# One written order for the first two batches of a fused attention, gated convolution and spatial-gating kernel

## The chip, the cores and the metric

The kernel runs on one core of a Trainium2 chip. The metric is the device time of one launch in microseconds (us). The core has a matrix engine (TensorE, "PE" in the profile; its weight loads are "PEld"), a vector engine (VectorE, "DVE"), an activation engine (ScalarE, "ACT"), a general engine (GpSimd, "POOL") and a queue that only issues DMA transfers here (SyncE, "SP"). Each engine works through its own list of instructions in the order of the list and waits on semaphores for the others.

## The reference

Three layers follow each other. Everything is float32, with 8 batches of 576 tokens.

```python
# 1: linear attention, 8 heads of 64
kv  = einsum('bhsd,bhse->bhde', k, v)
out = einsum('bhsd,bhde->bhse', q, kv)
rms = sqrt(mean(out * out, axis=-1, keepdims=True) + 1e-06)
x   = (out / rms * g_norm)            # -> (batch, 576, 512)
# 2: gated projection; the gate is a causal convolution with 5 taps
gate = 1 / (1 + exp(-sum_k conv_w[k] * shifted(x, k)))
y    = (gate * (x @ w_val)) @ w_out
# 3: spatial gating
h = gelu_tanh(y @ w_in);  u, v = split(h)
v_n = (v - mean(v)) / sqrt(var(v) + 1e-06) * g_ln
v_s = einsum('ts,bsd->btd', w_sg, v_n) + b_sg
return y + (u * v_s) @ w_out2
```

## The kernel before

Tokens of a batch are worked in five tiles of 128 (`TOK`; the fifth overlaps the fourth, its last 64 tokens, the "rest", are new). Layers 1 and 2 go batch by batch; layer 3 follows for all batches and is not touched. All matrix products keep float32 accuracy by splitting an operand into a high part (rounded to fp32r) and a low part (what is left): `gemm3` (line 222) makes 12 products of 128x512 for one output block of 128 columns.

One batch of layers 1 and 2 is this chain. `kv` makes the 8 head products k'v, 40 small matmuls; `kv_out` copies them on ACT into the block diagonal tile `kvbd`. For each token tile, `o` (line 291) multiplies q by `kvbd` into a PSUM bank `o`; ACT squares it (line 302); DVE sums over a head (305); GpSimd forms mean plus epsilon (306) and its power -0.5 (307), the "root" of 8 heads per token; DVE multiplies the bank by the root, broadcast over 64 columns (310, the "scale"). `transpose` turns the tile on PE into a bank `xT` (325), ACT writes the high part `X0h` or `X1h` (329) and the full float32 copy `X` (330), DVE the low part (334). `taps` and `conv` build the gate: ACT makes the first tap (353), DVE the other four (359), for each of four blocks of 128 channels; ACT takes the sigmoid (362). `Moe.val` (line 378) makes the product with w_val, DVE multiplies it by the gate (387), ACT writes the high part of `Z` (388), and the low part of `Z` (391) comes from GpSimd for blocks 0 and 2 and from DVE for blocks 1 and 3, save in batch 0, where DVE makes all four. `Moe.out` makes the product with w_out into a bank `y`, ACT copies it (405) and a DMA stores it.

The weights w_val, w_out and conv_w come in as float64 and are unpacked by DVE and ACT (lines 131 to 143); w_val and w_out need three steps more for their low parts, on PE and ACT for five of the eight column pieces (`summed`, tile `l`), on DVE for the other three (lines 186 and 188).

The order of the work is set in two ways. Up to the low parts of batch 0's `Z` it is written out by hand: the block under `tc.manual_schedule()` (line 705), where `busy(n)` puts n dummy matmuls of 128x128 (tile `warm`) on PE. After that, `later` and `tick` say in which slot a piece is due, and a scheduler orders each engine's list. SP's list starts with the four pieces of w_val, one of w_out, k and v of batch 0 in halves, conv_w and q. Batch 1's projections start while batch 0's `y` is under way.

Of the kernel before, what the change touches and what calls it, by code (L numbers as in the profile page):

```python
# [19 lines left out]
P = 128  # L20
# [8 lines left out]
KC = 5  # L29
# [6 lines left out]
ROOM = {"st": 128, "bst": 32, "bmv": 32, "gcol": 32, "gln": 32, "mhalf": 96, "cw": 64, "T": S, "X32": 19 * 128}  # L36
APART = 8

# [27 lines left out]
def body(ctx, tc, qT, k, v, gcol, w_val, conv_w, w_out, w_in, g_ln, w_sgT, b_sg, w_out2, out, out_r):  # L66
# [45 lines left out]
    nc.gpsimd.memset(mhalf, -0.5)  # L112
    kvbd = [sb(f"kvbd{i}", [NK, P]) for i in range(2)]
# [31 lines left out]
    def split(src, h, l, raw=None, tmp=None, k=None, last=nc.gpsimd.tensor_tensor):  # L145
# [20 lines left out]
        def first():  # L166
            if wide:
                st["steps"] = wide_parts(st["raw"].rearrange("p (n t) -> p n t", t=2),
                                         sb("cv", [3, n]) if tmp is None else tmp)
                st["steps"][0]()  # L170

        def steps():

            ops = st["steps"][1]
            yield ops[0]()
            yield ops[1]()
            a = ops[2]()
            act(h, flat(a), AF.Copy)
            yield
            yield ops[3]()  # L180
            c = ops[4]() if last else ops[4](l, flat)
            yield
            if last is None:
                st["parts"] = a, c
                return
            last(flat(a), flat(a), f32(h), op=ALU.subtract)  # L186
            yield
            tt(l, flat(a), flat(c), op=ALU.add)  # L188
            yield

        def summed():

            a, c = st["parts"]
            ps = bank("l", n)
            for i, (w, x) in enumerate(((ident, flat(a)), (signed[:, 1], h), (signed[:, 0], c))):
                nc.tensor.matmul(flat(ps), lhsT=w, rhs=x, start=(i == 0), stop=(i == 2))
            return lambda: act(l, flat(ps), AF.Copy)

        def rest():
            r = st["raw"]  # L200
            if wide:
                for _ in steps():
                    pass
            else:
                act(h, flat(r), AF.Copy)
                tt(l, flat(r), f32(h), op=ALU.subtract)
# [5 lines left out]
        return load, work, first, steps if wide else lambda: iter([rest()]), summed if wide and last is None else lambda: lambda: None  # L212
# [32 lines left out]

    class Attention:
        def __init__(self, b):
            self.b = b
            self.xh, self.xl = (sb(f"X{b % 2}{i}", [NK, MAIN], F32R) for i in "hl")

        def load_kv(self):
            b = self.b
            self.k, self.v = sb("K", [5, D]), sb("V", [5, D])
            for c in (((0, 2), (2, 4)) if b == 0 else ((0, 4),)):
                for t_, src in ((self.k, k), (self.v, v)):
                    dma(t_[:, c[0]:c[1], :], src[b, P * c[0]:P * c[1], :].rearrange("(c p) d -> p c d", p=P))
            dma(self.k[:, 4, :], k[b, TOK[4]:, :])
            dma(self.v[REST:, 4, :], v[b, MAIN:, :])
            nc.gpsimd.memset(self.v[:REST, 4, :], 0.0)

        def load_q(self):
            self.q = sb("Q", [NK, S])
            dma(self.q, qT[self.b].rearrange("m p s -> p m s"))

        def kv(self, half):
            if half == 0:
                if self.b:
                    pk = bank("kv")
# [13 lines left out]
            if half:  # L282
                later(0, self.kv_out, 0)

        def kv_out(self):
            bd = kvbd[self.b % 2]
            for pk, j in self.pk3:
                act(bd[:DH, j, :DH], pk[:DH, :, :DH], AF.Copy)
                act(bd[DH:, j, DH:], pk[DH:, :, DH:], AF.Copy)

        def o(self, t, wait=3):
            bd = kvbd[self.b % 2]
            o = TOK[t]
            po = bank("o")
            for j in range(NK):
                nc.tensor.matmul(po[:, j * P:(j + 1) * P], lhsT=self.q[:, j, o:o + P], rhs=bd[:, j, :], start=True, stop=True)  # L296
            st = sb("st", [3, 8], bufs=5)
            xo = tmp(D)
            x3 = xo.rearrange("p (h d) -> p h d", d=DH)

            def square():
                act(xo, po, AF.Square)

            def norm(small=nc.gpsimd.tensor_scalar):
                nc.vector.tensor_reduce(st[:, 0], x3, axis=AX.X, op=ALU.add)
                small(st[:, 1], st[:, 0], 1.0 / DH, 1e-6, op0=ALU.mult, op1=ALU.add)  # L306
                nc.gpsimd.tensor_tensor(st[:, 2], st[:, 1], mhalf, op=ALU.pow)  # L307

            def scale():
                tt(x3, po.rearrange("p (h d) -> p h d", d=DH),  # L310
                   st[:, 2].unsqueeze(2).to_broadcast([P, 8, DH]), op=ALU.mult)

            if wait is None:
                square()
                return norm, scale, lambda: self.transpose(t, xo, True)
            later(0, square, 0)
            later(0, norm, 0)
            later(wait - 1, scale, 0)
            later(wait, lambda: self.transpose(t, xo), 0)

        def transpose(self, t, xo, apart=False):
            o, n = (TOK[t], P) if t < 4 else (MAIN, REST)
            pt = bank("xT")
            for j in range(NK):
                nc.tensor.transpose(pt[:, j * P:(j + 1) * P], xo[:, j * P:(j + 1) * P], ident)
            pt = pt.rearrange("p (j e) -> p j e", j=NK)[:, :, P - n:]
            if t < 4:
                xh, xl = self.xh[:, :, o:o + n], self.xl[:, :, o:o + n]
                act(xh, pt, AF.Identity, scale=gcol_s)
            act(x32[:, :, HALO + o:HALO + o + n], pt, AF.Identity, scale=gcol_s)  # L330

            def low():
                if t < 4:
                    stt(xl, pt, gcol_s, f32(xh), op0=ALU.mult, op1=ALU.subtract)

            if apart:
                return low
            low()

        def rest_parts(self):  # L340

            if self.b % RG == 0:
                rest["x"] = sb("XR", [2, NK, RW], F32R, o=APART)
                rest["g"] = sb("GR", [NK, RW])
            c = self.b % RG * REST
            xs = x32[:, :, HALO + MAIN:]
            xh, xl = (rest["x"][:, i, :, c:c + REST] for i in range(2))
            act(xh, xs, AF.Copy)
            tt(xl, xs, f32(xh), op=ALU.subtract)
            act(rest["g"][:, :, c:c + REST], gate[:, :, MAIN:], AF.Sigmoid)  # L350

        def taps(self, m):
            act(gate[:, m], x32[:, m, 0:S], AF.Copy, scale=cw3[:, m, 0:1])  # L353

        def conv(self, ms):

            for j in range(1, KC):
                for m in ms:
                    stt(gate[:, m], x32[:, m, j:j + S], cw3[:, m, j:j + 1], gate[:, m], op0=ALU.mult, op1=ALU.add)  # L359
# [11 lines left out]
    class Moe:  # L371


        def __init__(self, xh, xl, g, dst):
            self.xh, self.xl, self.g, self.dst, self.n = xh, xl, g, dst, xh.shape[2]

        def val(self, m, apart=False):
            n = self.n
            if m == 0:
                self.z = sb("Z", [2, NK, n], F32R, o=APART if n == RW else 0)  # L380
            zh, zl = self.z[:, 0, m], self.z[:, 1, m]
            ps = bank("val", n)
            gemm3(ps, (wv[:, 0], wv[:, 1]), m, self.xh, self.xl)
            z = tmp(n)

            def gated():
                tt(z, ps, self.g[:, m, :n], op=ALU.mult)  # L387
                act(zh, z, AF.Copy)

            def low(on_pool=m in (0, 2)):  # L390
                (nc.gpsimd.tensor_tensor if on_pool else tt)(zl, z, f32(zh), op=ALU.subtract)  # L391

            if apart:
                return gated, low
            later(0, gated, 0)
            later(0, low, 0)

        def out(self, m):
            if m == 0:
                self.y = sb("Y", [NK, self.n])  # L400
            ps = bank("y", self.n)
            gemm3(ps, wo, m, self.z[:, 0], self.z[:, 1])

            def done():
                act(self.y[:, m], ps, AF.Copy)
                if m == NK - 1:
                    dma(self.dst, self.y)

            later(0, done, 1)
# [219 lines left out]
    def product():  # L629

        return next(i for i in reversed(nc.cur_bb.bb.instructions) if i.engine == mybir.EngineType.PE)
# [45 lines left out]
    wv_pieces = first_weight((wv[:, 0], wv[:, 1]), w_val, [first[0][:, i] for i in range(4)], tmps, [None] * 4)  # L677
    wo_pieces = first_weight(wo, w_out, [spare[:, 0], spare[:, 1], first[0][:, 0], first[0][:, 1]],
                             tmps[:2] * 2, [None, tt, tt, tt])
    att = Attention(0)  # L680
    atts = [att, Attention(1)]

    def taps():
        if conv_w.dtype == F32:
            dma(cw, conv_w)
            return lambda: None
        raw = sb("raw", [WC * 2], I32, bufs=2)[:, :2 * NK * KC]
        dma(raw, conv_w.bitcast(I32))

        def work():  # L690
            one, ops = wide_parts(raw.rearrange("p (n t) -> p n t", t=2), sb("cv", [3, NK * KC]))
            one()
# [292 lines left out]
```

## Time and profile before

| quantity | value |
|---|---|
| device time, median of 3 runs | 729.43 us (729.15 to 729.48) |
| time of the profiled execution | 727.04 us |
| its span, first to last instruction | 725.2 us |
| PE busy | 709.9 us, 98% |
| DVE busy | 583.6 us, 80% |
| ACT busy | 350.3 us, 48% |
| POOL busy | 152.5 us, 21% |
| granted TensorE clock | 1.000 (2.4 GHz) |

The span lies 1.8 us inside the profiled execution's time, and that execution 2.4 us under the median. Busy time is a sum over stages with different limits; the stretch that the change touches is the first 107 us or so, up to the first projection of batch 2 at 106.81 us. A record "x60" of 128x128 matmuls stands for 30 of them: each float32 product leaves two.

### The profile page before, as it was taken

Reading aid. Unit: us, or ns where it says so; the run is one execution under the profiler, and the core shown is the slowest. Engines: PE = TensorE matmul, PEld = TensorE weight load, DVE = VectorE, ACT = ScalarE, POOL = GpSimd, SP = SyncE. Lnnn points to the kernel's source line nnn. Section 1 sums busy time; section 2 is a strip of 40 time slices with the busy share of each in tenths; the row PEclk is TensorE's granted clock in tenths of the full one; section 3 lists DMA queues with packets and bytes.
Section 4 is the critical chain, followed back from the end, with each engine's and each line's share of the span. In section 5 each row is a group of like instructions: output and inputs, shape, how many; then the busy total and the mean of one; then the engine's idle time right before and its main releaser. Section 6 shows DMA issues by size and latency. Waiting matters only on the chain.

```text
span 725.2 us, 11759 instructions
## 1 busy us (share of the span) xinstructions
PE 709.9 (98%) x4490; PEld 620.7 (86%) x4490; DVE 583.6 (80%) x1127; ACT 350.3 (48%) x667; POOL 152.5 (21%) x173
## 2 busy tenths in 40 slices
PE   8997999999999999999999999999999999999998
PEld 7785888879888888899889889898899898898897
DVE  6699979999989999699976866867856857867662
ACT  4667465676566674475433433424333424334230
POOL 1414437262727361112000000000100000100000
PEclk9999999999999999999999999999999999999999
DMA  9945253525462213433220321122241122111202
GB/s 338 331 141 201 96 195 119 217 80 207 130 251 84 88 30 125 158 120 103 73 81 36 103 89 30 58 88 74 78 156 30 58 88 74 58 59 45 102 1 87
DMA packets 56712, 81.19 MB, mean 112 GB/s; under 512 B 3665, under 2 KB 29265, under 8 KB 55633
## 3 DMA queue, kind: packets, MB, share of 16 engines
q1 hardware_dynamic: 56656, 80.45, 32.2%
q8 instruction: 35, 0.57, 0.3%
q14 instruction: 21, 0.16, 0.1%
HBM read 61.56 MB, written 18.87 MB: 111 GB/s over the span
## 4 chain that ended last, share of the span: by engine, by line
PE 58%; DVE 1%; DMA 0%; ACT 0%; POOL 0%; issue 0%; POOLq 0%; SPq 0%; DVEq 0%
PE sg L587 16%; PE hv L478 14%; PE out L228 14%; PE hu L228 12%; PE hur L228 2%; PE y L228 1%; PE val L228 1%; DMA raw<-y_main 0%; DVE Z L391 0%; DVE T L387 0%; POOL cv L186 0%; DVE cv L134 0%; DVE V L188 0%; DVE cv L141 0%; ACT X1h L455 0%
## 5 line engine op out<-in xcount | busy, mean ns | idle before, releaser
L359 DVE SCALAR_TENSOR_TENSOR G<-X,cw,G 128x576 f32<-128x576 f32 x128 | 98.3, 819 | 5.2 <-ACT G L353 5.1
L228 PE MATMUL y<-Z,WOh 128*128 128x512 f32 (+1 forms) x320 | 96.8, 376 | 0.0
L490 POOL TENSOR_TENSOR bmv<-bmv,mhalf 128x1 f32<-128x1 f32 x36 | 21.4, 596 | 342.6 <-DVE bmv L489 342.6
L478 PE MATMUL hv<-wiv,X1h 128*128 128x512 f32 x256 | 83.1, 390 | 0.1
L228 PE MATMUL out<-Z,K 128*128 128x512 f32 x256 | 83.0, 389 | 0.0
L228 PE MATMUL hu<-X1h,wiu 128*128 128x512 f32 x256 | 79.2, 391 | 0.0
L307 POOL TENSOR_TENSOR st<-st,mhalf 128x8 f32<-128x8 f32 x40 | 70.2, 1762 | 7.0 <-DVE st L306 4.7
L228 PEld LDWEIGHTS y<-Z,WOh 128*128 128x128 f32 x320 | 57.9, 188 | 9.6
L467 ACT ACTIVATE T<-T 128x512 f32<-128x512 f32 x68 | 42.9, 631 | 44.7 <-DVE T L464 44.7
L228 PE MATMUL y<-Z,WOl 128*128 128x512 f32 (+1 forms) x160 | 57.9, 369 | 0.0
L228 PEld LDWEIGHTS out<-Z,K 128*128 128x128 f32 x256 | 48.1, 188 | 10.0
L478 PEld LDWEIGHTS hv<-wiv,X1h 128*128 128x128 f32 x256 | 47.8, 188 | 10.0 <-ACT X1h L455 0.5
L588 DVE SCALAR_TENSOR_TENSOR T<-sg,gln,WOl 128x288 f32<-128x288 f32 x64 | 32.7, 515 | 26.3 <-PE sg L587 26.2
L228 PEld LDWEIGHTS hu<-X1h,wiu 128*128 128x128 f32 x256 | 46.6, 188 | 8.3
L228 PE MATMUL hu<-X1l,wiu 128*128 128x512 f32 x128 | 50.0, 390 | 0.0
L478 PE MATMUL hv<-wiv,X1l 128*128 128x512 f32 x128 | 49.9, 390 | 0.0
L228 PE MATMUL out<-Z,V 128*128 128x512 f32 x128 | 49.8, 389 | 0.0
L599 ACT ACTIVATE Z<-T 128x512 fp32r<-128x512 f32 x32 | 20.1, 630 | 57.5 <-DVE T L598 57.5
L296 PEld LDWEIGHTS o<-kvbd,Q 128*128 128x128 f32 x320 | 40.3, 191 | 2.5 <-issue 0.3
L296 PE MATMUL o<-kvbd,Q 128*128 128x128 f32 x320 | 40.7, 275 | 0.1
L228 PE MATMUL val<-X0h,WV 128*128 128x512 f32 x128 | 40.7, 399 | 0.0
L228 PE MATMUL val<-X1h,WV 128*128 128x512 f32 x128 | 40.6, 398 | 0.0
(174 smaller groups left out, 1699.4 us busy)
## 6 DMA issues: line engine op xcount, KB each, us to landing
Q<-in_qT_dram SPq DMA_DIRECT2D x8, 1152.0 KB, 5.4
y_main<-Y SPq DMA_DIRECT2D x8, 1024.0 KB, 3.8
raw<-y_main SPq DMA_DIRECT2D x32, 256.0 KB, 3.1
Y<-y_main SPq DMA_DIRECT2D x32, 256.0 KB, 4.1
out_dram<-Y SPq DMA_DIRECT2D x32, 256.0 KB, 2.3
K<-in_k_dram SPq DMA_DIRECT2D x7, 1024.0 KB, 5.6
V<-in_v_dram SPq DMA_DIRECT2D x7, 1024.0 KB, 8.5
raw<-in_w_in_dram SPq DMA_DIRECT2D x16, 256.0 KB, 4.7
```

What stands on the lines that cost most here:

```text
L228: nc.tensor.matmul(ps, lhsT=a[:, kt, msl], rhs=x[:, kt], start=(i == 0), stop=(i == 3 * NK - 1))
L296: nc.tensor.matmul(po[:, j * P:(j + 1) * P], lhsT=self.q[:, j, o:o + P], rhs=bd[:, j, :], start=True, stop=True)
L307: nc.gpsimd.tensor_tensor(st[:, 2], st[:, 1], mhalf, op=ALU.pow)
L359: stt(gate[:, m], x32[:, m, j:j + S], cw3[:, m, j:j + 1], gate[:, m], op0=ALU.mult, op1=ALU.add)
L467: act(w, w, AF.Tanh, scale=CG * AG)
L478: nc.tensor.matmul(ps, lhsT=a[:, kt], rhs=p2["wiv"][:, w, kt], start=(i == 0), stop=(i == 3 * NK - 1))
L490: nc.gpsimd.tensor_tensor(mv[:, 3:4], mv[:, 2:3], mhalf[:, 0:1], op=ALU.pow)
L587: nc.tensor.matmul(ps, lhsT=a[:, msl], rhs=w, start=(n == 0), stop=(n == len(mm) - 1))
L588: later(0, lambda: stt(vs[:, sl], ps, gln_s[:, m:m + 1], p2["bsg"][:, sl], op0=ALU.mult, op1=ALU.add))
L599: act(g[:, 0], x, AF.Copy)
```

## The change

The block written by hand is replaced by a string `ORDER` of 356 tokens that are played one after the other, each one instruction or a few, on whichever engine it belongs to. The string reaches further than the old block: over both batches 0 and 1, up to the four `y` products of batch 0 and the low parts of batch 1's `Z`; batch 2's k'v, `o`, scales and transposes are in it too. A token names the step, then batch and tile: `o01` product, `q01` square, `r01` sum, `m01` mean, `w01` root, `s01` scale, `t01` transpose, `h01`, `x01`, `l01` high, full and low copy, `p021` tap 1 of block 2 in batch 0, `v01` the product with w_val, `z01`, `Z01`, `u01` its gated product, high part and low part, `y01` and `Y01` the output product and its copy. `a` and `b` tokens are steps of the weights, `L` tokens loads, `~n` puts n dummy matmuls ahead, and a star chooses the other engine: GpSimd for `m` and `u`, ACT for `s`.

Four things differ in what is done. Ten of the 15 scales in the string run on ACT as 8 activations of 128x64 each, one per head, with the root as the per-partition scale. Seven of the 8 low parts of `Z` of batches 0 and 1 run on GpSimd. Four of the means run on ACT. Four of batch 0's eight copies into `kvbd` run on DVE. There are 37 dummy matmuls in place of 51. Loads move: k and v of batch 0 come behind two pieces of w_val, q of batch 0 in two parts right behind them, the other weight pieces after q; the loads of batches 2 and 3 are issued inside or right at the end of the string, batch 3's q with its k and v.

```diff
+ORDER = """
+W30 La0 La1 LK0a LV0a LK0b LV0b LK0c LV0c Lq0a Lq0b Lg La2 La3 Lb0 Lcw a1a a0a a01 a00 a10 kv0a a02 a11 a12 kv0b a13
...
+p132 w24 t23 b3h b3s s24* w22 t21 p113 p133 s22* b3+ p102 p134 y03 p114 Y02 s20* g1L S11 h23 p103 v10 h21 z11 p104
+z12 l21 Z11 t22 S13 Z12 z13 S10 l23 Z13 h22 t24 z10 u11* t20 Z10 l22 u12* u10 h20 u13* x21 Y03 x23 x24 l20 x22 x20
+g1r
+"""
...
+    def own(ps):
+        for i in range(idle[0]):
+            nc.tensor.matmul(ps[:, :P], lhsT=ident, rhs=ident, start=True, stop=True)
+        idle[0] = 0
+        return ps
...
+        def mean(self, t, by=None):
+            st = self.tile[t]["st"]
+            if by is act:
+                act(st[:, 1], st[:, 0], AF.Identity, scale=1.0 / DH, bias=eps)
+            else:
+                nc.gpsimd.tensor_scalar(st[:, 1], st[:, 0], 1.0 / DH, 1e-6, op0=ALU.mult, op1=ALU.add)
...
+        def scale(self, t, by=None):
+            i = self.tile[t]
+            if by is act:
+                for h in range(8):
+                    act(i["x3"][:, h], i["po"][:, h * DH:(h + 1) * DH], AF.Copy, scale=i["st"][:, 2, h:h + 1])
+                return
+            tt(i["x3"], i["po"].rearrange("p (h d) -> p h d", d=DH),
+               i["st"][:, 2].unsqueeze(2).to_broadcast([P, 8, DH]), op=ALU.mult)
...
+        def low(self, m, on_pool):
             zh, zl = self.z[:, 0, m], self.z[:, 1, m]
...
+            (nc.gpsimd.tensor_tensor if on_pool else tt)(zl, self.t[m], f32(zh), op=ALU.subtract)
...
+        for op in ORDER.split():
+            op, n = (op + "~0").split("~")[:2]
+            idle[0] = int(n)
+            if op[0] == "L":
+                load(op[1:])
+            elif op[0] == "W":
+                busy(int(op[1:]))
+            elif op in ("kv0a", "kv0b"):
+                atts[0].kv("ab".index(op[3]), False)
+            else:
+                act_part(op.rstrip("*"), op[-1] == "*")
+    marks = [latest()] * 4
+    atts.append(Attention(3))
+    atts[3].load_kv()
+    atts[3].load_q()
```

SP's list at the start of the program, before: `wiu` receives w_val, `Y` w_out, `K`, `V` and `Q` are k, v and q of a batch.

```order
L164 DMA wiu_91<-in_w_val_dram 128x4x256 x4
L164 DMA Y_93<-in_w_out_dram 128x4x256
L256 DMA K_106<-in_k_dram 128x2x512
L256 DMA V_107<-in_v_dram 128x2x512
L256 DMA K_106<-in_k_dram 128x2x512
L256 DMA V_107<-in_v_dram 128x2x512
L257 DMA K_106<-in_k_dram 128x512
L258 DMA V_107<-in_v_dram 64x512
L688 DMA raw_115<-in_conv_w_dram 128x40
L263 DMA Q_117<-in_qT_dram 128x4x576
```

SP's list at the start, after:

```order
L183 DMA wiu_93<-in_w_val_dram 128x4x256 x2
L308 DMA K_137<-in_k_dram 128x2x512
L308 DMA V_138<-in_v_dram 128x2x512
L308 DMA K_137<-in_k_dram 128x2x512
L308 DMA V_138<-in_v_dram 128x2x512
L311 DMA K_137<-in_k_dram 128x512
L313 DMA V_138<-in_v_dram 64x512
L320 DMA Q_146<-in_qT_dram 128x4x256
L320 DMA Q_146<-in_qT_dram 128x4x320
```

Two pieces of w_val and the piece of w_out have gone behind q, and the first `o` product needs only q's first part.

ACT's list where batch 1's `Z` is made, before. `G` is the gate, `X0h` and `X` the copies of batch 2's transposed tiles, `T` a temporary, `GR` the rest's gate; line 302 is the square, 362 the sigmoid, 388 the high part of `Z`.

```order
L362 ACTIVATE G_86<-G_86 128x512
L329 ACTIVATE X0h_548<-xT_924,gcol_79 128x4x128
L388 ACTIVATE Z_834<-T_848 128x512
L302 ACTIVATE T_923<-o_917 128x512
L362 ACTIVATE G_86<-G_86 128x512
L330 ACTIVATE X_12_85<-xT_887,gcol_79 128x4x128
L330 ACTIVATE X_12_85<-xT_924,gcol_79 128x4x128
L350 ACTIVATE GR_615<-G_86 128x4x64
L388 ACTIVATE Z_834<-T_879 128x512
L388 ACTIVATE Z_834<-T_916 128x512
L388 ACTIVATE Z_834<-T_956 128x512
```

ACT's list ahead of the same `Z` after; line 385 is the scale, 511 the copy of `y`, 466 the sigmoid, 402 the high copy, 493 the high part of `Z`.

```order
L385 ACTIVATE T_751<-o_732,st_750 128x64 x8
L385 ACTIVATE T_761<-o_701,st_760 128x64 x8
L511 ACTIVATE Y_870<-y_891 128x512
L385 ACTIVATE T_766<-o_745,st_765 128x64 x8
L466 ACTIVATE G_88<-G_88 128x512
L402 ACTIVATE X0h_966<-xT_907,gcol_81 128x4x128
L402 ACTIVATE X0h_966<-xT_923,gcol_81 128x4x128
L493 ACTIVATE Z_990<-T_984 128x512
L466 ACTIVATE G_88<-G_88 128x512
L493 ACTIVATE Z_990<-T_987 128x512
```

All five scales of batch 2's tiles now stand on ACT ahead of batch 1's `Z`; the full copies `X` of batch 2, which stood between, have moved behind it.

## Rows read from the trace of the kernel before

**Rows 1.** Busy time by stretch: start:end, length, us busy (x instructions), clock, DMA.

```profile
0.00:21.86 21.86, 19.46 (x188) 17.24 (x189) 12.53 (x31) 10.70 (x23) 3.22 (x14) 1.00 0.94 333
0.00:93.15 93.15, 84.33 (x759) 72.13 (x759) 79.60 (x142) 56.50 (x106) 32.79 (x41) 1.00 0.62 221
30.00:92.00 62.00, 56.09 (x499) 47.89 (x499) 59.08 (x95) 40.34 (x74) 21.89 (x23) 1.00 0.47 166
106.00:320.00 214.00, 211.05 (x1434) 181.81 (x1433) 199.55 (x362) 131.83 (x255) 94.17 (x91) 1.00 0.38 135
320.00:725.00 405.00, 401.62 (x2237) 356.03 (x2235) 295.87 (x612) 153.01 (x291) 21.86 (x38) 1.00 0.22 72
```

**Rows 2.** PE's waits over the whole span: total us, times, longest.

```profile
PE xT L325 <- DVE T L310: 5.9, 7, 2.9
PE warm L244 <- POOL X L234: 2.3, 1, 2.3
PE xT L325 <- ACT WOh L178: 1.9, 1, 1.9
```

**Rows 3.** Timeline of PE: start, us, instruction, [idle before <- releaser].

```profile
15.02 1.60 PE L244 MATMUL warm<-ident 128*128 128x128 f32 x12
20.70 4.70 PE L296 MATMUL o<-kvbd,Q 128*128 128x128 f32 x40
...
64.62 0.66 PE L325 MATMUL xT<-ident,T 128*128 128x128 f32 x4 [2.87 <-DVE T L310]
...
93.15 0.48 PE L228 MATMUL y<-Z,WOh 128*128 128x512 f32 x1
...
106.81 0.71 PE L228 MATMUL val<-X0h,WV 128*128 128x512 f32 x2
```

**Rows 4.** The chain that ended last, one piece: 12 products of 128x512.

```profile
299.52 2.78 PE hv L478 x12
```

**Rows 5.** ACT's start: a piece of w_val; the first square of batch 0.

```profile
8.64 0.69 ACT L131 ACTIVATE Z<-wiu 128x512 f32<-128x512 f32 x1 [0.73 <-DMA wiu<-in_w_val_dram]
...
21.86 0.60 ACT L302 ACTIVATE T<-o 128x512 f32<-128x512 f32 x1 [1.82 <-PE o L296]
```

**Rows 6.** SP: the issue that waits for w_out's piece.

```profile
9.99 0.38 SPq L263 DMA_DIRECT2D Q<-in_qT_dram  x1
```

**Rows 7.** ACT by line and shape: busy us, mean ns of one.

```profile
L302 ACT ACTIVATE T<-o 128x512 f32<-128x512 f32 x40 | 23.3, 592 | 7.5 <-PE o L296 7.5
L330 ACT ACTIVATE X<-xT,gcol 128x512 f32<-128x512 f32 x32 | 21.8, 685 | 0.0
L599 ACT ACTIVATE WOh<-T 128x64 fp32r<-128x64 f32 x32 | 7.7, 241 | 0.0
```

**Rows 8.** Timeline of ACT: squares and small copies, back to back.

```profile
51.32 2.05 ACT L302 ACTIVATE T<-o 128x512 f32<-128x512 f32 x4
...
17.94 0.22 ACT L288 ACTIVATE kvbd<-kv 64x64 f32<-64x64 f32 x1 [1.28 <-PE kv L280]
18.16 0.22 ACT L289 ACTIVATE kvbd<-kv 64x64 f32<-64x64 f32 x1
18.41 0.22 ACT L288 ACTIVATE kvbd<-kv 64x64 f32<-64x64 f32 x1
```

**Rows 9.** DVE by line and shape: the scale, the low part of Z.

```profile
L310 DVE TENSOR_TENSOR T<-o,st 128x512 f32<-128x512 f32 x40 | 27.2, 682 | 2.7 <-POOL st L307 2.5
L391 DVE TENSOR_TENSOR Z<-T,Z 128x512 fp32r<-128x512 f32 x18 | 12.0, 680 | 0.0
```

**Rows 10.** Timeline of POOL (a low part) and of DVE (one weight step, twice).

```profile
115.67 1.30 POOL L391 TENSOR_TENSOR Z<-T,Z 128x512 fp32r<-128x512 f32 x1 [1.17 <-ACT Z L388]
...
116.16 0.95 DVE L143 TENSOR_SCALAR cv<-cv 128x256 int32<-128x256 int32 x1
...
128.17 0.28 DVE L143 TENSOR_SCALAR cv<-cv 128x256 int32<-128x256 int32 x1
```

More of the change, by code (lines that the diff above doesn't have):

```diff
@@ L201, in rest @@
             if wide:
-                for _ in steps():
-                    pass
+                steps()
             else:
@@ L304, in norm @@
[L304 to L315, printed above, removed]
@@ new lines, in full, with low, o @@
+        def full(self, t):
+            act(self.at(t), self.tile[t]["pt"], AF.Identity, scale=gcol_s)
+        def low(self, t, by=None):
+            xh, xl = (x[:, :, TOK[t]:TOK[t] + P] for x in (self.xh, self.xl))
+            if by is None:
+                stt(xl, self.tile[t]["pt"], gcol_s, f32(xh), op0=ALU.mult, op1=ALU.subtract)
+            else:
+                nc.gpsimd.tensor_tensor(xl, self.at(t), f32(xh), op=ALU.subtract)
+        def o(self, t, wait=3):
+            self.product(t)
+            later(0, lambda: self.square(t), 0)
+            later(0, lambda: self.sums(t), 0)
+            later(0, lambda: self.mean(t), 0)
+            later(0, lambda: self.root(t), 0)
+            later(wait - 1, lambda: self.scale(t), 0)
+            later(wait, lambda: self.transpose(t), 0)
@@ L398, in out, with product @@
-        def out(self, m):
[L399 to L409, printed above, removed]
+            self.ps, self.t, self.z, self.y, self.left = {}, {}, None, None, NK
+        def product(self, m):
+            self.ps[m] = own(bank("val", self.n))
+            gemm3(self.ps[m], (wv[:, 0], wv[:, 1]), m, self.xh, self.xl)
@@ new lines, in val, with out_product, done @@
+        def val(self, m):
+            self.product(m)
+            later(0, lambda: (self.gated(m), self.high(m)), 0)
+            later(0, lambda: self.low(m, m in (0, 2)), 0)
+        def out_product(self, m):
+            self.ps[m] = own(bank("y", self.n))
+            gemm3(self.ps[m], wo, m, self.z[:, 0], self.z[:, 1])
+        def done(self, m):
+            if self.y is None:
+                self.y = sb("Y", [NK, self.n])
+            act(self.y[:, m], self.ps[m], AF.Copy)
+            self.left -= 1
+            if not self.left:
+                dma(self.dst, self.y)
@@ L412, in body @@
+        def out(self, m):
+            self.out_product(m)
+            later(0, lambda: self.done(m), 1)
     p2 = {}
```

429 lines of the change are left out of this document (232 added, 197 removed).

## The prediction

> **What bounds the kernel now.** I read the busy time by stretch first. From 106 us on PE is busy 211.05 of 214 us and then 401.62 of 405 [rows 1]: what comes after the changed stretch is PE's, and a lead won before it is carried to the end. The changed stretch is another matter. PE's waits [rows 2] add up to some 11 us over the span, and the long ones are in its first 65 us: 2.3 before its first matmul, 1.9 for a weight step, 2.87 in one piece at 64.62 for a scale of DVE [rows 3]. The reader is to see that the releaser is DVE most of the time, and that DVE is the full engine there: 59.08 of 62 us between 30 and 92, with PE at 56.09 and ACT at 40.34 [rows 1]. So the change takes work from the fullest engine and gives it to one that is two thirds full. The chain that ended last does not help here; it shows PE alone.
>
> I measure the change at one mark. Before, batch 2's first product with w_val starts at 106.81 [rows 3]; what PE has done by then is the same set of products in both orders. In the new order the last thing ahead of it that waits for other engines is batch 1's first `y`, which needs the high part of `Z` block 0, the last of the four on ACT. Behind that stand four `y` of 12 products, 2.78 each [rows 4], and two `o` of 0.94 (4.70 for five [rows 3]): 13.0 us. Without a wait in them, the lead is 106.81 - 13.0 = 93.8 less the time at which that `y` starts.
>
> **The start.** The first `o` before waits behind 6.1 MB of loads (2.0 w_val, 0.5 w_out, 2.4 k and v, 1.15 q), after behind 3.9 (1.0, 2.4, 0.5 of q). Half a megabyte takes 1.35 us, from a piece of w_val at 8.64 [rows 5] to the next at 9.99 [rows 6]; 2.2 MB are 5.9 us. The first square moves from 21.86 [rows 5] to about 16.0. The weight pieces that come later in exchange are needed only at the `l` products behind the five `o`.
>
> **What ACT gains in work.** By 93.15, where batch 1's `y` starts before [rows 3], ACT has worked 56.50 us [rows 1]. The new list has 1.8 less ahead of it (two full copies of batch 2, the rest's gate, one copy of `y` and one of `kvbd` behind it, one high copy ahead), and 0.9 less for four small copies given to DVE. It has four means more, 0.2 each by the 0.22 of a small copy [rows 8], 0.8. And ten scales of eight activations of 128x64.
>
> No such activation with a per-partition scale is in the trace, so it is bounded. A 128x64 one without such a scale takes 0.241 [rows 7]; one with it is 0.093 longer (685 against 592 ns for 128x512 out of PSUM [rows 7]): 0.33 alone. Four squares back to back take 2.05 and not 2.37 [rows 8], so neighbours overlap by 0.1: 0.23. But the small copies into `kvbd` follow each other at 0.23 with 0.22 of length [rows 8], with no overlap. Ends: 0.22 to 0.33. I take 0.24, since full-width pieces overlap and the copies that don't change partitions at every step: 1.92 a scale, 19.2 for ten. The Trainium skill, "ScalarE: Activation LUTs", section "What ACT_TABLE_LOAD costs", gives 186 ns + 0.833 a column, 93 more for a pointer operand and 93 of overlap; its estimate would be 0.24 too, and the trace agrees on the length (241 ns).
>
> Sum: 56.5 - 1.8 - 0.9 + 0.8 + 19.2 = 73.8 us. Of the 10.70 that ACT has done before the first square [rows 1], nine weight steps of about 0.58 and five small ones move behind it, so 4.4 are done at 16.0 and 69.4 remain. That is now nearly all the time there is. How full can a list be that three engines wait on? DVE's was, at 59.08 of 62, 95%. At 95% the 69.4 take 72.8, and batch 1's `y` starts at 16.0 + 72.8 = 88.8, say 89.0 with the hop to PE.
>
> **The other engines at that mark.** DVE had worked 79.60 by 93.15 [rows 1]. It loses eight scales (13 of 15 were done by then, five are left) at 0.60, which is 682 ns [rows 9] less the overlap: 4.8; low parts of `Z`, net 2.0 at 680 ns [rows 9]; five small means, 1.0 by the length of a 128x64 piece [rows 7]; it gains four copies, 0.8, and a low copy, 0.7: 73.3, or about 1 us ahead of ACT at the same fill. PE had 84.33 [rows 1]; 14 dummies at 0.27 (1.60 for six [rows 3]) go, 3.7, two transposes come, 0.8: 81.4 and the 2.3 at its start [rows 2], 83.7. So both have slack of 1 to 5 us against ACT, and the waits that PE loses come back as shorter ones ahead of 89: ACT is late next. GpSimd makes five more low parts of 1.30 [rows 10], 6.5 us, on an engine that was busy 21.89 of 62 [rows 1]; `Z` is read one step later there, behind other products of PE.
>
> Those low parts touch DVE too. While GpSimd made one, from 115.67 to 116.97, a weight step of DVE that takes 0.28 took 0.95 and ended with it [rows 10]. I count nothing for it: in the new order most of the low parts lie beside DVE steps that read PSUM, and DVE has that 1 us. The other end is below. The Trainium skill, "SBUF — State Buffer", section "SBUF: two separate sides", calls the ports that the two engines share an exclusive lock, held for a whole instruction, against DVE steps with two SBUF inputs or in a two-port mode; by that rule each of the seven would cost DVE up to its whole length, and these rows agree with it.
>
> **Loads of batches 2 and 3.** q of batch 3 is now issued with its k and v, ahead of w_in's first pieces, all in SP's list. None is waited for within 10 us, and the DMA share falls below 0.4 behind 106 us [rows 1]; I count nothing, and up to 1 us if q comes late.
>
> **Sum.** 93.8 - 89.0 = 4.8 us. The profiled execution took 727.04 with a span of 725.2, so 722.2 for it; the median of the runs is 2.4 higher, 729.43, and 4.8 off that is 724.6.
>
> **Rivals.** *The order packs better than 95%.* If ACT never waits behind its first square, `y` starts at 16.0 + 69.4 = 85.4, still behind PE's 83.7; the lead is 8.4, the time 721.0. For it: the string places every step by hand, and PE's own bound allows it. Against: DVE, waiting on the same chains, got no further than 95%. 20%.
>
> *The small activations don't overlap* (the slower side). The place is ACT's list between the squares and `Z`; the price is 0.33 in place of 0.24, 80 times, 7.2 us, or 7.6 at that fill. `y` starts at 96.6, 2.8 later than now, and the time is 732.2. It decides from 0.24 + 4.8 x 0.95 / 80 = 0.30 each on: there the whole lead is gone. For it: the only small pieces in the trace follow at their full length. Against: those alternate between partition halves. 15%.
>
> *GpSimd's lock slows DVE.* Seven low parts, each holding a DVE step by 0.67 as in rows 10, 4.7 us: DVE's 73.3 become 78.0, and with about 5 done by 16.0 it ends at 16.0 + 73.0 / 0.95 = 92.8. Lead 1.0, time 728.4. For it: the taps have both operands in SBUF. Against: two such parts a batch cost far less before. 8%.
>
> *PE's clock falls.* With 37 dummies for 51, PE pauses more in the first 35 us. In the trace it stood still for 2.87 us [rows 3] and the granted clock stayed 1.00 in every stretch shown [rows 1], the higher of the two levels; I see no pause longer than that in the new order. If it fell once, 5 us of matmuls would take 10: 730 or so. 5%. That the change does not do what it says is excluded by the instruction lists.
>
> **How the numbers follow.** Forecast 47%, the four rivals 48%, 5% for what I don't see. The range runs from the better packing, 721.0, to between the lock and the missing overlap, 731.0. Its own range for the forecast is 722.5 to 727 (ACT filled to 97 or 92%, 0.23 to 0.26 an activation). No change, within 0.2% or 1.5 us, is about what a measurement here can tell. Faster: the packing 20, the forecast 46, the lock 2, the rest 4: 72%. Same: 13%, from the lock and small overlaps. Slower: 15%.
>
> **What would show it.** Right: the first square near 16, ACT over 90% busy from 25 to 88, scales of 1.9 us, batch 1's `y` near 89, PE's waits ahead of it for ACT. Wrong: eight activations taking 2.4 us or more; DVE taps of 1.2 us and more beside GpSimd's low parts; PE waiting for DVE or GpSimd at that `y`; a clock under 1.00; or a lead at 107 us that is gone by 320.

## The result and the profile after

| | before | after |
|---|---|---|
| median of the runs, us | 729.29 (727.91 to 729.48, 4 runs) | 718.46 (718.32 to 719.03, 4 runs) |
| profiled execution, us | 727.04 | 718.38 |
| span, us | 725.2 | 716.6 |

The ratio is 0.986, 95% interval 0.9844 to 0.9876: 10.8 us less, where the prediction said 4.8. The two profiled executions differ by 8.7.

Busy time by stretch in the changed kernel (start:end, length, us busy, clock, DMA), up to the first square, up to batch 1's first `y`, the middle, and from the first square to the end of batch 1's last high part of `Z`, against [rows 1]:

```profile
0.00:16.80 16.80, 14.60 (x154) 13.92 (x154) 5.53 (x14) 4.00 (x9) 3.27 (x15) 1.00 0.92 306
0.00:87.36 87.36, 83.90 (x738) 71.78 (x738) 73.15 (x131) 70.53 (x186) 44.86 (x50) 1.00 0.67 224
30.00:86.00 56.00, 55.84 (x464) 48.10 (x461) 55.41 (x93) 53.35 (x147) 31.81 (x26) 1.00 0.52 173
16.80:85.58 68.78, 67.52 (x528) 56.14 (x529) 66.23 (x115) 64.75 (x174) 41.49 (x35) 1.00 0.63 209
```

The columns behind the length are the busy times of PE, its weight loads, DVE, ACT and POOL. In the middle three engines are full at once: PE 55.84, DVE 55.41 and ACT 53.35 of 56 us. Before it was DVE alone. PE's waits over the whole span, against [rows 2]:

```profile
PE xT L394 <- DVE T L387: 2.1, 5, 0.9
PE warm L282 <- POOL ident masks.py:199: 1.9, 1, 1.9
PE o L358 <- ACT kvbd L349: 0.3, 1, 0.3
```

From some 11 us they have fallen to under 5; the piece of 2.87 us is gone, the longest behind the start is 0.9. PE's timeline at the places of [rows 3], and one behind the mark:

```profile
1.85 9.88 PE L282 MATMUL warm<-ident 128*128 128x128 f32 x60 [1.85 <-POOL ident masks.py:199]
...
15.61 5.07 PE L358 MATMUL o<-kvbd,Q 128*128 128x128 f32 x40 [0.28 <-ACT kvbd L349]
...
87.36 0.50 PE L266 MATMUL y<-Z,WOh 128*128 128x512 f32 x1
...
100.09 0.71 PE L266 MATMUL val<-X0h,WV 128*128 128x512 f32 x2
...
139.10 0.63 PE L394 MATMUL xT<-ident,T 128*128 128x128 f32 x4 [0.20 <-DVE T L387]
```

Batch 1's `y` starts at 87.36 with no wait ahead of it, and the mark stands at 100.09: a lead of 6.72 us. On ACT, by line and shape, against [rows 7], and one scale in its timeline, against [rows 8]:

```profile
L364 ACT ACTIVATE T<-o 128x512 f32<-128x512 f32 x40 | 23.3, 595 | 9.2 <-PE o L358 9.1
L405 ACT ACTIVATE X<-xT,gcol 128x512 f32<-128x512 f32 x32 | 21.6, 703 | 0.0
L385 ACT ACTIVATE T<-o,st 128x64 f32<-128x64 f32 x80 | 17.3, 382 | 0.0
```

```profile
22.61 1.76 ACT L385 ACTIVATE T<-o,st 128x64 f32<-128x64 f32 x8
```

One scaled activation of 128x64 is 0.382 us long, but eight take 1.76 and 80 take 17.3: 0.216 each, since each overlaps its neighbour by almost half.

Behind the mark the lead grows. Before, batch 3's first transpose waited 1.30 us for DVE, which was busy 39.26 of the 40.44 us up to there:

```profile
147.25 0.63 PE L325 MATMUL xT<-ident,T 128*128 128x128 f32 x4 [1.30 <-DVE T L310]
```

```profile
106.81:147.25 40.44, 38.98 (x279) 33.28 (x278) 39.26 (x69) 24.10 (x46) 22.01 (x20) 1.00 0.45 163
```

In the changed kernel the same products take 39.01 us with DVE at 34.91, and the wait is the 0.20 above:

```profile
100.09:139.10 39.01, 38.82 (x279) 33.24 (x278) 34.91 (x65) 23.85 (x46) 21.26 (x20) 1.00 0.48 169
```

The lead there is 8.15, at 320 us 8.2, at the end 8.6.

### The profile page after: what moved, and what is told of

Read it like the earlier page. It is cut to its first block, busy times and chain, and to the rows that moved or that the text cites. A ratio compares the mean times of both kernels' runs of the same rounds, so it can differ in the third digit from the quotient of the medians.

```text
span 716.6 us, 11759 instructions
## 1 busy us (share of the span) xinstructions
PE 708.3 (99%) x4462; PEld 619.6 (86%) x4462; DVE 572.5 (80%) x1111; ACT 365.4 (51%) x747; POOL 160.7 (22%) x180
## 4 chain that ended last, share of the span: by engine, by line
PE 82%; DVE 12%; DMA 2%; ACT 1%; issue 1%; POOL 1%; SPq 0%; DVEq 0%; POOLq 0%
PE sg L696 17%; PE hv L587 14%; PE out L266 14%; PE hu L266 12%; PE y L266 11%; PE val L266 8%; DVE G L457 6%; PE o L358 2%; PE hur L266 2%; PE xT L394 1%; PE kv L337 1%; DVE st L368 1%; DMA V<-in_v_dram 1%; DMA wiu<-in_w_val_dram 1%; DVE T L387 1%
## 5 line engine op out<-in xcount | busy, mean ns | idle before, releaser
L379 POOL TENSOR_TENSOR st<-st,mhalf 128x8 f32<-128x8 f32 x40 | 72.9, 1833 | 2.7
```

## The experiments

All times are medians of four to ten executions; each was run beside the kernel before. The changed kernel run again gave 718.57 and 718.71, so differences are taken from 718.6. A "dose" is work added or moved to see where it shows. In the diffs of `ORDER` only the tokens that differ and some neighbours stand; "..." marks what is left out. A "fall" is a stretch in which the granted TensorE clock is below 1.00.

**The base once more** (e1): the kernel before, with no edit.

> The kernel before, unchanged, profiled and timed once more. Open: its profiled execution took 727.04 us, 2.2 below its median of 729.29, while the changed kernel's profiled 718.38 is its median. (a) Executions of the kernel before fall on two lengths, and the profile caught a short one: single times spread from 727 to 729.5, and a new profile may take about 729, with the 2 us visible as waits. (b) The gap is a property of profiling this kernel: profiled again 727.0 to 727.3, timed 729.3. Under both, the ratio to itself is 1.000 within 0.2%.

727.95 against 727.88, ratio 1.0004 (0.9991 to 1.0017). This profiled execution took 730.17 with a span of 728.4, 3.2 above the first one; 0.56 of that stands ahead of the wait (its transpose starts at 65.18 for 64.62). Windows of 3 us around the wait of 2.87, and PE's timeline there:

```profile
63.00:66.00 3.00, 0.82 (x5) 0.82 (x5) 3.00 (x7) 1.72 (x3) 1.35 (x1) 0.73 0.60 223
66.00:69.00 3.00, 3.00 (x9) 2.40 (x8) 3.00 (x7) 2.41 (x4) 0.00 (x0) 0.50 0.00 0
69.00:72.00 3.00, 3.00 (x13) 2.29 (x12) 3.00 (x6) 0.59 (x2) 0.00 (x0) 0.63 0.00 0
72.00:75.00 3.00, 3.00 (x23) 2.78 (x22) 2.04 (x4) 2.97 (x7) 0.00 (x0) 1.00 0.03 5
```

```profile
65.18 1.12 PE L325 MATMUL xT<-ident,T 128*128 128x128 f32 x4 [2.87 <-DVE T L310]
...
66.94 1.05 PE L228 MATMUL y<-Z,WOh 128*128 128x512 f32 x2
...
78.47 0.62 PE L228 MATMUL y<-Z,WOh 128*128 128x512 f32 x2
```

The granted clock falls from 1.00 to 0.50, the lower level, with the same 2.87 us wait that left it at 1.00 in the first profile; two products take 1.05 us in place of 0.62 until about 71 us. So (a) holds: this kernel has executions with and without a fall. Of 58 executions of it on five chips 14 show a mean clock of 1.000 (median 727.4), 39 show 0.997 or 0.998 (728.1) and five 0.995 or 0.996 (730.1). The changed kernel shows 1.000 in 12 of 12 (718.2 to 719.1, median 718.6). That a mean clock of 0.997 is the same fall, only shorter, is not shown: no profile was taken of such an execution of the kernel before.

**The two moves undone** (e2, e3, e6).

```diff
-s01* s11* s13* s10* s12* s23* s21* s24* s22* s20*
+s01 s11 s13 s10 s12 s23 s21 s24 s22 s20
```

> The changed kernel with all 15 scales on VectorE, the order otherwise as it is. ACT loses 17.3 us of work in its first 87 us, VectorE gets ten steps of 0.60, 6.0 us. If VectorE is the fullest engine of the new stretch (55.41 of 56 us busy between 30 and 86), the time rises by the 6.0: 724.5. If TensorE bounds it (55.84 of 56) and VectorE has a slack of 2 us or so, by about 4: 722.5. If ACT were the limiter, as the prediction had it, the time would not rise: 717.5 to 718.5.

724.0 (723.03 to 724.73), 5.4 above the changed kernel; 723.0 and 723.3 in the two runs with a clock of 1.00, 4.6 above. That is between VectorE's full price and TensorE's slack, and no sign of an ACT that limits the whole stretch.

```diff
-u00* u01* u03* u02* u11* u12* u13*
+u00 u01 u03 u02 u11 u12 u13
```

> The changed kernel with all eight low parts of z of the written stretch on VectorE. VectorE gets seven steps of 0.60 to 0.68, 4.2 to 4.8 us, four of them behind batch 1's y or just ahead of it. If VectorE is the bound: 722.5 to 723. If TensorE is, with 2 us of slack on VectorE: 720 to 721. If GpSimd's low parts hold VectorE by as much as they spare it (the lock of the prediction's rival), nothing changes: 718.5.

721.36, 2.8 above. The lock theory falls. Most of it is one wait of PE, at batch 0's last `y`, for a bank that one of ACT's scales of batch 2 frees, late behind a DVE that has more to do:

```profile
PE y L266 <- ACT T L385: 2.0, 1, 2.0
```

Both together:

> The changed kernel with all 15 scales and all eight low parts of z on VectorE: the written order, the earlier first o and fewer dummies alone. VectorE gets 6.0 and 4.2 us. If the two moves add up as they did one by one (4.6 and 2.5 us above the changed kernel), 725.5: the order and the start are worth 2 to 3 us by themselves and the moves 7. If the order alone brings nothing, 727.5 to 728, as before. If VectorE has a slack that one move's undoing had already used, the sum is higher than 7: 727 to 729.

725.69 (724.87 to 726.81), ratio 0.9968 (0.9955 to 0.9981): 7.1 above the changed kernel, 1.1 less than the two one by one (5.4 and 2.8), and 2.1 below the kernel before. In the three runs with a clock of 1.00 it is 6.7 above, against 4.6 and 2.8. Its profile shows what becomes of the earlier start without the moves:

```profile
30.00:86.00 56.00, 51.56 (x400) 42.87 (x397) 55.92 (x94) 33.40 (x65) 26.21 (x19) 1.00 0.52 173
```

```profile
93.52 0.50 PE L266 MATMUL y<-Z,WOh 128*128 128x512 f32 x1
```

DVE is busy 55.92 of 56 us, and batch 1's `y` starts at 93.52, behind the 93.15 of the kernel before, though the first `o` started at 15.87 for 20.70. The lead is 0.40 at the mark and 2.1 at the end: what e6 wins, it wins behind the mark. It still has the order, the loads, fewer dummies, four means on ACT and four copies into `kvbd` on DVE; of these only the loads (e10) and the dummies (e7, e12) were tested alone.

**The moves without the order** (e9): in the kernel before.

```diff
             def scale():
+                if (self.b, t) in ((0, 1), (1, 0), (1, 1), (1, 2), (1, 3), (2, 0), (2, 1), (2, 2), (2, 3), (2, 4)):
+                    for h in range(8):
+                        act(x3[:, h], po[:, h * DH:(h + 1) * DH], AF.Copy, scale=st[:, 2, h:h + 1])
+                    return
...
-            def low(on_pool=m in (0, 2)):
+            def low(on_pool=m in ((1, 2, 3) if self is moes[0] else (0, 2))):
...
-            z[m][1](False)
+            z[m][1](True)
```

> The kernel before, in its own order, with the same ten scales on ACT and the same seven low parts of z on GpSimd. Undoing the moves in the changed kernel cost 7.1 us, the order alone brought 2.1. If the moves bring their 7 in any order, since VectorE is relieved by 10 us of work: 720 to 722. If they need the order (ACT takes the scales where the scheduler puts them, and waits there for GpSimd's root with squares and copies behind it): 725 to 729.

734.35 (733.59 to 734.94), ratio 1.0083 (1.0068 to 1.0099): 6.2 slower than before, worse than either theory. DVE is relieved as meant, 53.88 of 62 us against 59.08 [rows 1], and gains nothing:

```profile
30.00:92.00 62.00, 57.53 (x443) 48.11 (x444) 53.88 (x82) 47.34 (x121) 26.23 (x24) 0.97 0.43 153
```

ACT's longest wait and DVE's two longest between 20 and 115 us (total, times, longest):

```profile
ACT T L312 <- POOL st L307: 4.7, 2, 4.0
DVE X0l L338 <- ACT X L334: 7.9, 3, 5.3
DVE st L305 <- ACT T L302: 4.9, 3, 3.6
```

ACT takes its list in order. A scale put into it ahead of time stands 4.0 us for GpSimd's root, and the copies and squares behind it make DVE wait 5.3 and 3.6. The same moves are worth +6.2 in this order and -7.1 in the written one. A part may be the clock: the 0.97 above is a fall (0.57 between 62 and 66 us), and all four runs show a mean clock of 0.993 to 0.997. Between runs at 0.997 on both sides the difference is still 5.9.

**Doses on each engine** (e4, e7, e8, e15). Ten dummies on PE, none of the seven, 12 and 8 scales on ACT:

```diff
-v00
+v00~10
```

> The changed kernel with ten dummy matmuls of 0.275 us put ahead of batch 0's first val product, 2.75 us of TensorE work that feeds nothing. If TensorE bounds the stretch from 30 us on, all of it shows: 721.2. If ACT or VectorE bounds it and TensorE has 1.5 to 2 us of slack by batch 1's y, 0.8 to 1.2 shows: 719.3 to 719.7, with ACT and VectorE as full as before.

```diff
-o01~3 t03~1 o21~3
+o01 t03 o21
```

> The changed kernel without its seven dummies behind o01, t03 and o21 (W30 stays). The first four stand in waits of TensorE (for q, for the scales of VectorE); the three of o21 stand where it waits for nothing else (0.16 us ahead of them), 0.77 us. If TensorE bounds the stretch from 30 us on: 0.7 less than the changed kernel beside it. If another engine does: no difference, within 0.2. If the clock hangs on the dummies: a granted clock under 1.00 and 1 us or more longer.

```diff
-s02 s00
+s02* s00*
```

> The changed kernel with 12 of 15 scales on ACT: two more of batch 0 (s02, s00), 1.2 us less on VectorE, 3.4 us more on ACT between 24 and 34 us, where ACT waits for nothing. If ACT is the limiter behind the first square, as the prediction had it, up to 3.4 longer than the changed kernel. If TensorE bounds it and ACT has slack, 0 to 0.5 longer. If VectorE is the limiter, 0.5 to 1.0 shorter.

```diff
-s12* s21*
+s12 s21
```

> The changed kernel with eight scales on ACT: s12 and s21 back on VectorE, 1.2 us more there, 3.5 less on ACT. With none on ACT the time was 724.0, with ten 718.5, with twelve 721.7. If VectorE sets the places where these two stand (s12 ahead of the X1l of batch 1 at 58 us): 719.3 to 720. If ACT does, as at 23 to 34 us where two more cost 3.3: 717.5 to 718.3.

Measured: 720.90, 718.50, 721.73 and 719.64, or +2.3, -0.1, +3.1 and +1.0. By scales on ACT: none 724.0, eight 719.6, ten 718.6, twelve 721.7. What the profiles show is where each dose lands, as the start of the same product less that in the changed kernel's first profile. In that kernel's own second and third profile the same starts differ by +0.90 and -0.41 at the first `o` and by +0.59 and +0.05 at the mark, so a value below 1 us in the table says little by itself:

| place (its start there) | ten dummies | none | 12 scales | all scales on DVE | lows on DVE |
|---|---|---|---|---|---|
| first `o` (15.61) | +0.28 | +0.51 | +0.27 | +0.42 | +0.54 |
| batch 1's first `o` (33.60) | +0.65 | +0.53 | +2.90 | +2.68 | +1.38 |
| second half of batch 0's `val` (47.86) | +2.92 | +0.55 | +3.34 | +2.70 | +1.40 |
| batch 1's `val` (60.66) | +2.47 | +0.07 | +3.46 | +4.60 | +1.16 |
| batch 0's last `y` (77.91) | +2.47 | +0.12 | +3.46 | +5.62 | +3.41 |
| the mark (100.09) | +2.49 | +0.19 | +3.43 | +6.38 | +3.43 |

The two scales more, 1.8 us each in ACT's list, are nearly all there by 48 us; from 26 us on ACT is busy 6.00 of 6 us:

```profile
25.32 1.81 ACT L385 ACTIVATE T<-o,st 128x64 f32<-128x64 f32 x8
...
29.25 1.89 ACT L385 ACTIVATE T<-o,st 128x64 f32<-128x64 f32 x8
```

```profile
26.00:32.00 6.00, 5.76 (x34) 3.73 (x36) 4.12 (x10) 6.00 (x22) 3.78 (x4) 0.72 1.06 340
```

The clock fell there too (0.72), but it is not what costs the 3.1: the two runs at a clock of 1.00 took 721.78 and 721.68. In the profile with all scales on DVE it also fell, behind waits of PE of 0.73, 0.96 and 0.25 us:

```profile
28.00:32.00 4.00, 4.00 (x14) 2.52 (x14) 3.94 (x10) 3.17 (x6) 2.62 (x2) 0.57 1.06 350
```

So the 2.68 of that column at 34 us is not a dose on DVE: only one scale, 0.7 us, has moved by then, and e6, with the same scale on DVE and a clock of 1.00, stands at 0.00 there. About 1.5 us of the column is the fall, by 724.7 for its two runs at 0.998 against 723.2 for the two at 1.00. The 1.38 of the last column stands ahead of its dose, which begins at 55 us, and is no effect of it.

At 48 the dummies (2.25 us of PE's time) show in full, and 0.43 of them is taken up at 56. The three dummies taken away at 56 win 0.8 there, and 0.3 of it is lost by the next `val`; the rest is as large as what the starts of two executions differ by, and the median shows nothing. Steps of this size inside a column are near the noise: the changed kernel's second profile made up 0.34 at the same place. So no single engine bounds the stretch: ACT binds at 24 to 34 us, PE at 48, and by the scales and low parts given back DVE behind that. Two of the four runs without the seven dummies show a mean clock of 0.997, at no cost that the median shows.

**What stands at 55 us** (e13, e14, e17, e18).

```diff
-Z00 g0L m14* t10 b21 t12 ... w14 b30 h10 ... o23 b22
+Z00 m14* t10 t12 ... w14 h10 ... o23 g0L b21 b30 b22
```

> The changed kernel with three steps of VectorE that nothing near waits for (the rest's low part g0L, weight steps b21 and b30: 0.42, 0.42 and 0.42 long, 1.1 us together) moved from ahead of batch 1's scale s14 and low parts X1l to behind them; the dummies stay. If TensorE alone bounds the stretch around 56 us (it waits 0.16 there and holds three dummies): 0.1 to 0.2 shorter, 718.4. If VectorE sets it: up to 1 shorter, 717.5.

The same and `o21` for `o21~3`:

> The same with the three dummies of o21 gone too. Without the dummies alone nothing was won, and in that trace batch 1's first val product started 0.38 us behind the last X1l of VectorE. If the two engines bound the place together (TensorE by the dummies, VectorE by what stands ahead of X1l), taking both away gives 0.7 to 0.9: 717.6 to 717.9, where either alone gives 0 to 0.2. If some later chain is late at once, as close to nothing as either alone: 718.4.

719.56 and 719.42: 1.0 and 0.8 longer, where every theory had them shorter or the same. DVE did not come earlier to the scale `s14`; the steps taken away had filled a wait for GpSimd's root (e14, DVE):

```profile
55.21 0.69 DVE L387 TENSOR_TENSOR T<-o,st 128x512 f32<-128x512 f32 x1 [0.84 <-POOL st L379]
```

In the next two (e17, e18) the low part of batch 0's rest is made from batch 1's values, since its step now stands behind the copy that overwrites them; their output is wrong, and they serve for times alone.

```diff
-Z00 g0L m14* t10 b21 t12 ... w14 b30 h10 ... o21~3 ... o23 b22 ... x12 b31 m23* w23 b23 b32 r22 ... r20 u02*
+Z00 m14* t10 t12 ... w14 h10 ... o21 ... o23 b21 b22 ... x12 m23* w23 b23 r22 ... r20 g0L b30 b31 b32 u02*
```

> The changed kernel without the dummies of o21, with VectorE's g0L, b30, b31 and b32 behind batch 2's last sum r20 and b21 behind X1l: no step now stands ahead of X1l, and batch 2's sums come earlier, not later. In e13 and e14 the 0.3 won at 58 us was lost again, 0.94 at batch 0's last y (77.9), which waited for a bank that ACT's scale of batch 2 frees. If the sums that were pushed back by 1.1 us did that, the loss is gone: 718.1 to 718.4. If it is the weight steps (b2, b3) that are late for that y, it stays: 719.3.

With `r14 z01` for `z01 r14` as well:

> The same with batch 1's last sum r14 one VectorE step (0.6 us) earlier. In e14 VectorE waited 0.84 for GpSimd's root of that tile ahead of the scale s14, and in the changed kernel the scale started 0.04 behind the root's end: by that the chain square, sum, mean, root sets batch 1's X1l, not the fullness of VectorE. If so, 0.4 to 0.6 shorter than e17: 717.6 to 717.9. If not, the same.

719.92 and 720.43 (719.87 to 724.48). The sums are not the cause of the loss. By its time e17 falls on the branch of the weight steps, but that is not what batch 0's last `y` waits for: it waits 0.98 for ACT's scale, as it waits 0.84 in e14. Whatever is taken from the filled wait stands later ahead of DVE's taps; these start at 67.98 in e17 and at 66.11 in the changed kernel, and a sigmoid in ACT's list waits for them, with the last scales of batch 2 behind it. In e13 and e14 0.6 of the delay is one weight step that takes 1.02 for 0.42 beside a low part of GpSimd. In the changed kernel:

```profile
72.53 0.63 ACT L466 ACTIVATE G<-G 128x512 f32<-128x512 f32 x1 [0.58 <-DVE G L457]
```

In e13 (in e17 the same wait is 2.64):

```profile
74.28 0.64 ACT L466 ACTIVATE G<-G 128x512 f32<-128x512 f32 x1 [1.95 <-DVE G L457]
```

In e18 `s14` did start 0.6 earlier, and the next step of DVE waited that much longer for ACT:

```profile
54.69 0.69 DVE L387 TENSOR_TENSOR T<-o,st 128x512 f32<-128x512 f32 x1 [0.25 <-POOL st L379]
...
56.34 0.75 DVE L410 SCALAR_TENSOR_TENSOR X1l<-xT,gcol,X1h 128x512 fp32r<-128x512 f32 x1 [0.95 <-ACT X L405]
```

By these waits four chains (PE's dummies, DVE's list, GpSimd's root, ACT's copies) end there within a microsecond of each other. None of the versions tried beats the changed kernel.

**Loads and the first dummies** (e10, e11, e12).

```diff
-W30 La0 La1 LK0a LV0a ... Lg La2 La3 Lb0 Lcw
+W30 La0 La1 La2 La3 Lb0 LK0a LV0a ... Lg Lcw
```

> The changed kernel with w_val's last two pieces and w_out's first loaded ahead of k, v and q again, 1.5 MB or 4.0 us at 1.35 per half megabyte; the order of the work stays. If the start carries to the end, as the prediction had it, the first o moves from 15.6 to 19.7 and the time rises by 3.5 to 4: 722 to 722.6. If the work behind it has slack that takes it up, 0 to 1: 718.5 to 719.5.

722.91, 4.3 longer; the first `o` moved by 4.59, and 4.04 of it is left at the mark. All four runs show a mean clock of 0.991 to 0.998, and the profile a fall (0.71) between 16 and 22 us, where PE had waited for v; what it adds is not separated.

```diff
     atts[3].load_kv()
-    atts[3].load_q()
...
-            if nn and s == 3:
+            if nn and s == (4 if b == 1 else 3):
                 nn.load_q()
```

> The changed kernel with the load of batch 3's q (1.15 MB) put back behind w_in's first pieces, at the step where the kernel before has it. The DMA engines are busy under half of the time there and nothing waits for q: no difference, within 0.3 us, by the prediction's count. If the early load is what keeps q out of a wait in batch 3's o, 0.5 to 1 longer, with TensorE waiting for Q.

```diff
-W30
+W20
```

> The changed kernel with 20 dummies ahead of the first product in place of 30. They end some 2 us earlier, but TensorE then waits for k and v: the time stays, within 0.3 us, if only the loads set the first kv. If the clock hangs on them, the granted clock falls below 1.00 in the first 30 us, and the time is 1 us or more longer.

718.61 and 718.72: no difference, as counted. In e12 the clock is 0.91 in the first 20 us, where PE then waits 2.2 us for v, and costs nothing, since loads set that stretch. One of four runs in each is longer, 723.72 and 722.07, at a mean clock of 0.995 and 0.993. So variants of the new order can meet a fall too, as in the profiles of e2, e8 and e10; the changed kernel itself has not, in its 12. A long pause is not needed for it: in the 10 us ahead of the fall in e2 no wait of PE was longer than 0.96 us, and e6, with waits of 0.50, 0.96 and 0.25 at the same place, kept 1.00.

The changed kernel itself, beside e6 to e8 and beside e13 to e15:

> The changed kernel, unchanged, once more beside the kernel before, as the base for the three runs beside it. The kernel before was found to take 727.3 to 728 us with the granted clock at 1.00, and 728.6 to 730.5 where it fell for some 6 us behind the 2.87 us pause at 64.6 us. If the part of the gain that the two profiles don't show (10.8 by the medians, 8.7 by the profiles) is that fall, the changed kernel, whose longest pause is 0.9, shows a clock of 1.00 in every run and the gain is 8.7 to 9.3 against runs of before without the fall. If it is something else, the gain is 10.8 against these too.

> The changed kernel as the base of the three runs beside it: 718.4 to 718.7, the granted clock at 1.00 in every run if its short waits are what spares it the fall that the kernel before shows; in one run of four or so 3 to 5 us longer, at a mean clock of 0.995 or less, if it is only rarer.

718.57 against 727.79, ratio 0.9872 (0.9855 to 0.9889); 718.71 against 727.85, 0.9871 (0.9856 to 0.9886). On these chips the gain is 9.2 and 9.1. Between the 14 runs of before at a clock of 1.00 (727.4) and the 12 of the changed kernel (718.6) it is 8.8.

## Why the prediction was wrong

The direction was right, the size was not: 4.8 of 10.8 us. The missing 6.0 are three terms of about 2.

**The lead at the mark, 6.72 for 4.8.** *The start* held: 16.80 for 16.0, and e10 moves the first `o` by 4.59 for 1.5 MB, where 1.35 per half megabyte gives 4.05. *The filling* held as well: ACT worked 64.75 of 68.78 us from the first square to the last high part, 94% for 95. What failed is *the work*, 69.4 predicted and 64.75 found. 1.9 of that is the scale, 17.3 for 19.2: I took 0.24 from overlaps of 0.1 seen at full width, and neighbours of 64 columns overlap by 0.17. The Trainium skill, "ScalarE: Activation LUTs", section "What ACT_TABLE_LOAD costs", gave 0.24 too, from 93 ns of overlap; the trace does not agree. The other 2.8 is overlap between ACT's lines, for which the sum has no term. Adding up ACT's busy times line by line leaves out that a step overlaps its neighbour of another line. Before, the lines sum to 60.6 us up to 93.15, and ACT was busy 56.5, 4.1 less; in the new list they sum to 78.9 up to 85.58, and it was busy 68.75, 10.2 less, since the steps now follow each other almost without gaps. Against these 6.1 stand 2.9 of work that I had not counted (the lines rose by 18.3, and by 15.4 in my sum with the scale at 17.3) and 0.4 less done before the first square (4.00 for 4.4). So ACT was done at 85.6, ahead of PE, whose bound, put at 83.7, was 87.36. Fourteen dummies fewer gave 1.8 and not 3.7 (14.0 us before, 12.2 after, as the first 30 took 9.88 for 8.42), and waits of 1.6 behind the start stayed where I had counted none. In the second and third profile the 30 took 8.68 and 8.74, but PE then waited 1.80 and 0.61 for v, and the mark came no earlier: there the loads bind. DVE's 73.3 held: 73.15 by 87.36. "ACT is late next" was wrong at that place, though e8 shows ACT in the way earlier, at 24 to 34 us.

**"A lead won before it is carried to the end": 8.7 by the profiles, not 6.7.** I read 211.05 of 214 us [rows 1] as PE's own and passed over the other 2.95. 1.1 of them was batch 3's wait for a DVE that still worked off batch 2. It goes with the order, also with the moves undone: in e6 that wait is 0.19. The other 0.8 of the growth is not traced.

**"The median of the runs is 2.4 higher", taken as a constant.** It was not one: for the changed kernel the two agree within 0.1. On the five chips where the clock of each run is known, about 0.5 of it goes with the lower clock that most executions of the kernel before show and its first profile did not (727.9 over all 58, 727.4 over the 14 at 1.00). The rest belongs to the first comparison alone: there the kernel before took 729.3, and 727.8 to 728.3 later, while the changed kernel took the same in all three. The clocks of those runs of before are not recorded, so that part stays open. The rival on the clock was put upside down: I looked for pauses that the change adds, and argued from one execution that 2.87 us do no harm. The kernel before had the longer pause, and 44 of its 58 executions show a lower mean clock. That this pause starts the fall in e1 is inferred from its place; a kernel before with the pause filled was not run, and e2 shows a fall behind shorter ones.

**The rivals.** *Packs better* was nearest in time (721.0), but not by its mechanism: ACT was no fuller than I said. *Small activations don't overlap* is refuted by the 0.216. *GpSimd's lock*: three low parts in a row on POOL, and DVE beside them:

```profile
81.88 3.80 POOL L497 TENSOR_TENSOR Z<-T,Z 128x512 fp32r<-128x512 f32 x3 [6.56 <-ACT Z L493]
...
114.14 1.28 POOL L497 TENSOR_TENSOR Z<-T,Z 128x512 fp32r<-128x512 f32 x1 [1.55 <-ACT Z L493]
```

```profile
82.31 0.74 DVE L410 SCALAR_TENSOR_TENSOR X0l<-xT,gcol,X0h 128x512 fp32r<-128x512 f32 x1
82.97 0.68 DVE L488 TENSOR_TENSOR T<-val,G 128x512 f32<-128x512 f32 x1
...
106.20 0.29 DVE L162 TENSOR_SCALAR cv<-cv 128x256 int32<-128x256 int32 x1
...
114.61 0.96 DVE L162 TENSOR_SCALAR cv<-cv 128x256 int32<-128x256 int32 x1
```

Steps that read PSUM are as long as ever; the weight step again takes 0.96 for 0.29 and ends 0.15 behind the low part, much as in [rows 10]. In e13, where a weight step was moved beside a low part, it took 1.02 for 0.42. In the changed kernel the steps beside the low parts ahead of the mark read PSUM or are sums, nearly all of them, so the count of nothing was right, and e3 says the move is worth 2.8.

## What to carry to other kernels

Moving work to a less busy engine is not a sum of busy times: ten scales and seven low parts were worth -7.1 us in a list written for them and +6.2 in the old one, because an engine that takes its work in order holds everything behind a step that comes too early. When a list is full on three engines at once, test it with doses on each at several places before trying to improve it: they show where each engine binds, and here none of the four reorderings tried won anything. Nor are busy times of a list with gaps the work of a full one: here steps of ACT that follow each other closely hid 6.1 us more in overlaps. And compare a profile's own time with the median on both sides, with the granted clock of each run and of each stretch: a median can hold falls that the one profile happens not to show, and a profile, as here those of two of the doses, one that the change did not bring.

## What was not expected of the hardware

- A scaled activation of 128x64 out of PSUM lasts 0.382 us and follows its neighbour after 0.216.
- The granted clock fell to 0.50 behind a wait of 2.87 us in one profiled execution and stayed at 1.00 behind the same wait in another; the fall lasted some 6 us, and the execution was 3.2 longer, 0.56 of it ahead of the wait.
- It also fell, to 0.50 at 28 us, behind waits of 0.73, 0.96 and 0.25 us in e2, and not behind waits of 0.50, 0.96 and 0.25 us in e6.
- The first 30 dummies took 8.42 us before, 9.88 in the changed kernel, 8.68 in its second profile, at a granted clock shown as 1.00. They last from 0.58 each at the start to 0.275 each later on. No run explains it; in the second profile PE waits 1.80 us for v soon behind them, so the loads hide it.
